# Side steps in another order, q's S1 rows copied from SBUF to SBUF, and the last outputs flushed in another order

## The chip, the cores and the metric

The kernel runs on one core of a Trainium2 chip. The metric is the time of one execution on the device in microseconds (us), the median of several runs. Before the change it is 363.53 us (three runs, 363.38 to 364.76). The engines are TensorE (PE; its weight loads are listed as PEld), VectorE (DVE), ScalarE (ACT), GpSimd (POOL) and SyncE (SP), which here issues the DMA transfers.

## The reference, cut to what matters

A linear attention with a quadratic feature map, and behind it a gated feed-forward block that mixes along the sequence. There are 4 batches, 4 heads, 1088 positions, head size 32 (128 features over the heads), R = 8, 512 gate features.

```python
def phi(x):                                    # 64 features of each position
    a = einsum('rd,bhsd->bhsr', S1, x)
    b = einsum('rd,bhsd->bhsr', S2, x)
    return einsum('bhsi,bhsj->bhsij', a, b).reshape(..., 64)
kv  = einsum('bhsf,bhsd->bhfd', phi(k), v);  z = sum_s phi(k)
x   = einsum('bhsf,bhfd->bhsd', phi(q), kv) / (einsum('bhsf,bhf->bhs', phi(q), z) + 1e-6)
# heads joined: x is [batch, 1088, 128]
h   = gelu(x @ w_in);  u, v = h[..., :512], h[..., 512:]
vn  = (v - mean(v)) / sqrt(var(v) + 1e-6) * g_ln
vs  = einsum('ts,bsd->btd', w_sg, vn) + b_sg[None, :, None]
out = x + (u * vs) @ w_out
```

## The kernel before, in words

Products that need precision are made as three matmuls of float32r halves (high by high, low by high, high by low). A few are plain float32 matmuls.

The work is a chain of batches. For each batch the **main loop** (`Gate.main`) goes over four feature blocks `db` of 128 and three chunks `ci` of the sequence (364, 362 and 362 columns). For each pair it makes `unit` (u, lines 380 to 382), and accumulates the spatial mixing over nine tiles `t` of the sequence in one PSUM bank (`pz`: lines 363, 365 and 371, 26 matmuls). Then `scale` (line 392) and `gate` (lines 400 to 406) make the gated product and its halves gh and gl on DVE and ACT. The gated product is put on a list `pend`; at `t == FL` (7) of each pair, the oldest entry is flushed: `out` multiplies it by w_out into `po` (lines 429 to 431). Four entries are on the list at a time. In the last block, `out` also adds x's two halves (lines 437 and 438) and stores the chunk (line 439). The very last pair of the whole program, `self.final`, is made in plain float32 with a joined weight `wf` (line 427) and one addition of a prepared `xs` (line 435).

While the main loop of batch b runs, the **side steps** of batch b + 1 are put between its matmuls (`Side`): `k1`, `k2` and `kv` (the features of k and their sums with v), `load_q`, `q1`, `q2`, `qp2` and `q3` (the features of q by chunk, and x), `v1`, `v2`, `v3` and `split` (the feed-forward's second half, its normalisation, and its halves vh and vl). Each step has a time in the table `FIRST` (batch 1, beside batch 0) or `LATER` (batches 2 and 3). The main loop calls `tick()` between groups of matmuls, and a step is emitted at the tick that its time falls on. The framework's scheduler then orders the instructions of each engine from there, so that a step can end up later than its tick. Batch 0's own first part, the **head**, runs before any main loop; there a list scheduler orders the steps by costs written in the program plus a correction for each of them in the table `HEAD`.

`spread` takes a chunk's 64 projected rows of q, `ab` (32 rows of S1, 32 of S2), and makes two tiles of 128 rows for each pair of heads: in one each S1 row stands 8 times in a row, in the other the 8 S2 rows of a head are repeated. `qp2` then multiplies the two on DVE (line 237), rounds the product on ACT (line 239) and has POOL make the low half (line 240). Before, `spread` writes both repeated forms to DRAM (lines 151 and 156) and loads them back (line 162).

The tiles of one tag share a fixed number of buffers, among them `r` 6, `ea` and `eb` 2, gt 4, gh and gl 3.

Of the kernel before, what the change touches and what calls it, by code (L numbers as in the profile page):

```python
# [9 lines left out]
F32 = mybir.dt.float32  # L10
# [7 lines left out]
B, H, S, D, R = 4, 4, 1088, 32, 8  # L18
P = 128
# [4 lines left out]
NB = DG // P  # L24
CH = [(0, 364), (364, 362), (726, 362)]
CW = 364
# [4 lines left out]
FL = 7  # L31
# [4 lines left out]


FIRST = [
# [6 lines left out]
]  # L45
LATER = [
# [5 lines left out]
]  # L52
HEAD = [
# [14 lines left out]
]  # L68


def f32(ap):
    return ap.bitcast(F32)
# [11 lines left out]
def tile_kernel(ctx: ExitStack, tc: tile.TileContext, qd, kd, vd, sd, wd, bd, wind, gd, woutd, identd, outd):  # L84
    nc = tc.nc
    mm = nc.tensor.matmul
    V, A, G = nc.vector, nc.scalar, nc.gpsimd
    load = nc.sync.dma_start

    cpool = ctx.enter_context(tc.tile_pool(name="const", bufs=1))  # L90
    dram = ctx.enter_context(tc.tile_pool(name="dram", bufs=1, space=bass.MemoryType.DRAM))
    psum = ctx.enter_context(tc.tile_pool(name="ps", bufs=3, space=PSUM))

    def const(shape, name, dt=F32):
        return cpool.tile(shape, dt, name=name)
# [35 lines left out]
    wout_h = const([P, NB, C], "wout_h", F32R)  # L131
    wout_l = const([P, NB, C], "wout_l", F32R)
# [14 lines left out]

    def spread(pool, ab, cw, name):

        d = dram.tile([2, 2, P, 3 * P], F32, tag="e", name=name + "d", bufs=3)  # L150
        load(
            d[0].rearrange("p (x j) c -> (p x) j c", j=R)[:, :, :cw],
            ab[:32, :cw].unsqueeze(1).broadcast_to([32, R, cw]),
        )
        for p in range(2):
            load(
                d[1, p].rearrange("(i x) c -> x i c", i=R)[:, :, :cw],
                ab[32 + 16 * p : 48 + 16 * p, :cw].unsqueeze(1).broadcast_to([16, R, cw]),
            )
        e = [pool([P, 2, 3 * P], "e" + x, name + x) for x in "ab"]  # L160
        for i in range(2):
            load(e[i][:, :, :cw], d[i].rearrange("p q c -> q p c")[:, :, :cw])
        return e

    class Attention:
# [108 lines left out]
    class Gate:  # L274
# [122 lines left out]
        def gate(self, pool, gt, u, db, ci):  # L397
            c0, cw = CH[ci]
            with tc.high_priority(AHEAD):
                V.tensor_mul(gt, gt, u)  # L400
                if (db, ci) == self.final:
                    return self, db, ci, gt, None
                gl = pool([P, CW], "gl", f"gl{self.b}_{db}_{ci}", F32R)[:, :cw]
                gh = pool([P, CW], "gh", f"gh{self.b}_{db}_{ci}", F32R)[:, :cw]
                A.copy(gh, gt)  # L405
                V.tensor_sub(gl, gt, f32(gh))  # L406
            return self, db, ci, gh, gl

        def end(self, db, ci):

            self.final = db, ci
            xh, xl = self.x
            c0, cw = CH[ci]
            self.wf = self.pool([P, C], "wf", "wout_f")
            V.tensor_add(self.wf, f32(wout_h[:, db]), f32(wout_l[:, db]))
            self.xs = self.pool([P, 512], "r", "x_f")[:, :cw]
            V.tensor_add(self.xs, f32(xh[:, c0 : c0 + cw]), f32(xl[:, c0 : c0 + cw]))

        def out(self, pool, db, ci, gh, gl):
            if db == 0 and ci == 0:  # L420
                self.po = [bank(f"po{self.b}_{c}", f"po{c}", 1) for c in range(3)]
            xh, xl = self.x
            c0, cw = CH[ci]
            cs = slice(c0, c0 + cw)
            o = self.po[ci][:, :cw]
            if (db, ci) == self.final:
                mm(o, lhsT=self.wf, rhs=gh, start=False, stop=True)
            else:
                mm(o, lhsT=wout_h[:, db], rhs=gh, start=(db == 0), stop=False)  # L429
                mm(o, lhsT=wout_l[:, db], rhs=gh, start=False, stop=False)  # L430
                mm(o, lhsT=wout_h[:, db], rhs=gl, start=False, stop=(db == NB - 1))  # L431
            if db == NB - 1:
                ot = pool([P, CW], "gt", f"o{self.b}_{ci}")[:, :cw]
                if (db, ci) == self.final:
                    V.tensor_add(ot, o, self.xs)
                else:
                    V.tensor_add(ot, o, f32(xh[:, cs]))
                    V.tensor_add(ot, ot, f32(xl[:, cs]))
                load(outd[self.b, :, cs], ot)

        def main(self, pool, tick, first, pend, extra=()):
            extra = list(extra)
            if first == 1:
# [3 lines left out]
                for i in range(2 * NT):  # L447
                    t = i % NT
# [8 lines left out]
                for ci in range(len(CH)):  # L457
                    gt = self.scale(pool, zs[ci], 1, ci)
                    u = us.pop() if us else self.unit(pool, 1, ci)
                    pend.append(self.gate(pool, gt, u, 1, ci))  # L460
                first = 2
            for db in range(first, NB):
                for ci in range(len(CH)):
                    cw = CH[ci][1]
                    u = self.unit(pool, db, ci)
                    z = bank(f"pz{self.b}_{db}_{ci}", "psn", 2)[:, :cw]
                    for t in range(NT):
                        self.spatial_h(z, db, ci, t)
                        self.spatial_l(z, db, ci, t)
                        if db + 1 < NB and ci == 0 and t in (1, 3, 5):  # L470
                            run(self.split(db + 1, 3 * (t // 2), 3))
                        if t == FL and pend:
                            flush(pool, *pend.pop(0))
                        if t in EX and extra:
                            extra.pop(0)()
                        if t < NT - 1:
                            tick()
                    pend.append(self.gate(pool, self.scale(pool, z, db, ci), u, db, ci))
                    tick()
# [135 lines left out]
    class Head:  # L615
# [7 lines left out]
        def load(self, name, kb, f, after=()):  # L623
            self.s.at(name, "SP", 0.47, f, after, late=-kb)
# [366 lines left out]
    pend = []  # L991
# [103 lines left out]
```

## Time and profile before

| | |
|---|---|
| median of 3 runs | 363.53 us (363.38 to 364.76) |
| the profiled execution | 363.2 us, of which 361.4 us are the span of the profile |
| PE busy | 350.6 us, 2022 matmuls |
| PE weight loads busy | 321.6 us |
| DVE / ACT / POOL busy | 249.3 / 162.4 / 22.0 us |
| DMA | 30.18 MB, of which 20.92 MB read from and 8.91 MB written to DRAM |

The profile is of one execution. Times in it count from the start of the span. A row of the timeline gives the start, the duration, the engine, the source line, the operation with its output and inputs, and in brackets how long the engine stood before it and what released it. A row of a group (a line, an operation, a shape) gives the count, the busy sum, the mean in ns, and the idle time before. A row of a stretch gives the busy time and the instruction count of each engine in it (PE, PEld, DVE, ACT, POOL), the granted clock of PE, the busy share of the DMA engines and GB/s. Matmuls are pipelined and their ends are modelled, so a busy PE is not a PE at its peak. A transfer's time to landing runs from its issue to its completion.

### The profile page before, as it was taken

Reading aid. Unit: us, or ns where it says so; the run is one execution under the profiler, and the core shown is the slowest. Engines: PE = TensorE matmul, PEld = TensorE weight load, DVE = VectorE, ACT = ScalarE, POOL = GpSimd, SP = SyncE. Lnnn points to the kernel's source line nnn. Section 1 sums busy time; section 2 is a strip of 40 time slices with the busy share of each in tenths; the row PEclk is TensorE's granted clock in tenths of the full one; section 3 lists DMA queues with packets and bytes.
Section 4 is the critical chain, followed back from the end, with each engine's and each line's share of the span. In section 5 each row is a group of like instructions: output and inputs, shape, how many; then the busy total and the mean of one; then the engine's idle time right before and its main releaser. Section 6 shows DMA issues by size and latency. Waiting matters only on the chain.

```text
span 361.4 us, 5443 instructions
## 1 busy us (share of the span) xinstructions
PE 350.6 (97%) x2022; PEld 321.6 (89%) x2022; DVE 249.3 (69%) x603; ACT 162.4 (45%) x355; POOL 22.0 (6%) x37
## 2 busy tenths in 40 slices
PE   7998999999999999999999999999999999999994
PEld 6875569898989999999898999999998999999993
DVE  4688799975999767636859866553697948553134
ACT  5466861325644963314545682332444593232110
POOL 0003000103101000022020000020202000000000
PEclk9999999999999999999999999999999999999998
DMA  7993000883500034484000007672000001000001
GB/s 228 395 410 120 1 2 21 189 260 82 139 21 2 0 82 130 146 206 170 2 0 0 23 0 166 146 191 78 2 0 1 2 0 38 25 0 2 0 2 62
DMA packets 18121, 30.18 MB, mean 84 GB/s; under 512 B 1968, under 2 KB 15024, under 8 KB 18096
## 3 DMA queue, kind: packets, MB, share of 16 engines
q1 hardware_dynamic: 18096, 29.84, 28.2%
q8 instruction: 16, 0.26, 0.3%
q14 instruction: 9, 0.07, 0.1%
HBM read 20.92 MB, written 8.91 MB: 83 GB/s over the span
## 4 chain that ended last, share of the span: by engine, by line
PE 81%; DVE 9%; ACT 5%; DMA 1%; issue 1%; SPq 1%; POOL 1%; DVEq 0%; ACTq 0%
PE pz L363 18%; PE pz L371 17%; PE pz L365 16%; PE pkv L193 3%; ACT vn L335 2%; PE pz L944 2%; PE pv L287 2%; PE pu L380 2%; PE po L431 2%; PE pk L178 2%; PE po L430 2%; PE po L429 2%; PE pv L288 1%; PE pv L289 1%; PE pu L382 1%; PE pu L381 1%
## 5 line engine op out<-in xcount | busy, mean ns | idle before, releaser
L363 PE MATMUL pz<-w_h,vh 128*128 128x362 f32 (+1 forms) x405 | 134.1, 333 | 0.2
L371 PE MATMUL pz<-w_l,vh 128*128 128x362 f32 (+1 forms) x405 | 129.6, 329 | 0.0
L365 PE MATMUL pz<-w_h,vl 128*128 128x364 f32 (+1 forms) x360 | 118.0, 328 | 0.0
L363 PEld LDWEIGHTS pz<-w_h,vh 128*128 128x128 f32 x405 | 76.0, 188 | 1.9 <-DVE gt L392 0.8
L371 PEld LDWEIGHTS pz<-w_l,vh 128*128 128x128 f32 x405 | 75.5, 188 | 0.3
L365 PEld LDWEIGHTS pz<-w_h,vl 128*128 128x128 f32 x360 | 67.7, 188 | 1.2 <-DVE vl L353 0.4
L392 DVE SCALAR_TENSOR_TENSOR gt<-pz,g_col,b_bc 128x362 f32<-128x362 f32 (+1 forms) x48 | 28.1, 590 | 53.7 <-PE pz L371 53.2
L405 ACT CAST gh<-gt 128x362 fp32r<-128x362 f32 (+1 forms) x47 | 22.9, 494 | 63.3 <-PE po L430 54.7
L385 ACT ACTIVATE u<-pu 128x362 f32<-128x362 f32 (+1 forms) x48 | 22.6, 473 | 23.9 <-PE pu L382 17.3
L335 ACT ACTIVATE vn<-vn,nm,rs 128x512 f32<-128x512 f32 x36 | 27.7, 809 | 9.2 <-DVE nm L330 7.5
L353 DVE TENSOR_TENSOR vl<-vn,vh 128x384 fp32r<-128x384 f32 (+2 forms) x60 | 23.1, 419 | 8.4 <-ACT vh L348 8.3
L400 DVE TENSOR_TENSOR gt<-gt,u 128x362 f32<-128x362 f32 (+1 forms) x48 | 25.7, 541 | 3.2 <-ACT u L385 2.9
L259 DVE RECIPROCAL den<-den 128x362 f32<-128x362 f32 (+1 forms) x9 | 21.8, 2417 | 8.8 <-ACT den L256 8.8
L348 ACT CAST vh<-vn 128x384 fp32r<-128x384 f32 (+1 forms) x63 | 23.1, 419 | 7.1 <-PE pz L371 7.1
L406 DVE TENSOR_TENSOR gl<-gt,gh 128x362 fp32r<-128x362 f32 (+1 forms) x47 | 24.6, 529 | 2.4 <-ACT gh L405 1.8
L292 ACT ACTIVATE vn<-pv 128x512 f32<-128x512 f32 x27 | 16.0, 599 | 14.8 <-PE pv L289 14.6
L944 PE MATMUL pz<-w_f,vn 128*128 128x362 f32 (+3 forms) x54 | 18.0, 476 | 1.4 <-ACT vn L335 1.4
L295 DVE BATCH_NORM_STATS2 st<-vn 128x6 f32<-128x512 f32 x27 | 17.9, 678 | 1.4 <-ACT vn L292 1.2
L944 PEld LDWEIGHTS pz<-w_f,vn 128*128 128x128 f32 (+1 forms) x54 | 9.8, 189 | 8.4 <-ACT vn L335 3.1
L380 PE MATMUL pu<-x_h,win_h 128*128 128x362 f32 (+1 forms) x48 | 16.7, 349 | 0.2 <-ACT u L385 0.2
L141 DVE TENSOR_TENSOR kp<-pk,kb 128x256 f32<-128x256 f32 x27 | 11.2, 421 | 7.8 <-ACT kb L181 5.6
L431 PE MATMUL po<-gl,wout_h 128*128 128x362 f32 (+1 forms) x47 | 15.8, 336 | 0.9 <-DVE gl L406 0.9
(195 smaller groups left out, 525.5 us busy)
## 6 DMA issues: line engine op xcount, KB each, us to landing
w_f<-in_w SPq DMA_DIRECT2D x9, 544.0 KB, 10.5
vx<-in_v SPq DMA_DIRECT2D x8, 288.0 KB, 5.0
k<-in_k SPq DMA_DIRECT2D x3, 576.0 KB, 6.2
out<-o SPq DMA_DIRECT2D x8, 181.0 KB, 3.0
e_0d<-ab SPq DMA_DIRECT2D x3, 364.0 KB, 4.4
e_0d<-ab SPq DMA_DIRECT2D x6, 182.0 KB, 5.2
e_0a<-e_0d SPq DMA_DIRECT2D x3, 364.0 KB, 4.1
e_0b<-e_0d SPq DMA_DIRECT2D x3, 364.0 KB, 4.3
```

The costliest lines, as they stand in the source:

```text
L335: A.activation(self.vn[:, t], self.vn[:, t], AF.Identity, bias=self.nm[:, t : t + 1], scale=self.rs[:, t : t + 1])
L348: A.copy(vh[:, ts], vs[:, ts])
L353: self.last = V.tensor_sub(vl[:, ts], vs[:, ts], f32(vh[:, ts]))
L363: last = mm(z, lhsT=vh[:, t], rhs=w_h[:, t, cs], start=(t == 0), stop=False)
L365: last = mm(z, lhsT=vl[:, t], rhs=w_h[:, t, cs], start=False, stop=False)
L371: mm(z, lhsT=self.parts[db][0][:, t], rhs=w_l[t][:, c0 : c0 + cw], start=False, stop=(t == NT - 1))
L380: mm(pu, lhsT=win_h[:, ws], rhs=xh[:, cs], start=True, stop=False)
L392: V.scalar_tensor_tensor(gt, z, g_col[:, db : db + 1], b_bc[:, c0 : c0 + cw], op0=ALU.mult, op1=ALU.add)
L400: V.tensor_mul(gt, gt, u)
L406: V.tensor_sub(gl, gt, f32(gh))
L431: mm(o, lhsT=wout_h[:, db], rhs=gl, start=False, stop=(db == NB - 1))
L944: return mm(zs[ci], lhsT=g.vn[r, t, :P], rhs=w_f[t][r, c0 : c0 + cw], start=(t == 0), stop=(t == NT - 1),)
```

## The change

Four things are changed together:

- the tables `FIRST`, `LATER` and `HEAD` have other numbers (67, 67 and 228 of them, as before);
- `spread` stores only the 32 S2 rows to DRAM, without repeating them; the S1 rows are copied from `ab` straight to the tile, repeated by the transfer; the S2 rows are repeated by the loads from DRAM;
- in the last block of the last batch, two entries of `pend` are flushed in each of the first two chunks and one in the third, so that two are left behind the last group of matmuls; the last batch's outputs are added in one addition each, with x's halves joined beforehand for all three chunks; the addition of chunk 1 is placed behind the final gate's multiplication on DVE;
- the last output is stored in two halves, one issued by SP and one by ACT.

```diff
 FIRST = [
-    8.367, 12.087, 9.623, 6.432, 6.419, 24.648, 11.799, 24.091, 14.517, 39.473, 17.629, 25.126, 22.662, 41.732,
+    -3.495, 11.694, 4.203, 5.044, 4.638, 28.588, 6.333, 23.954, 9.045, 33.842, 12.162, 19.634, 22.34, 36.212,
...
 LATER = [
-    -2.62, 3.464, 4.391, 10, 5.105, 23.019, 12.475, 12.486, 15.836, 11.397, 21.299, 13.02, 21.662, 15.404,
+    -3.752, 3.464, 4.373, 8.047, 3.772, 22.93, 12.437, 12.448, 17.015, 2.843, 19.477, 13.103, 19.806, 23.485,
...
     def spread(pool, ab, cw, name):
 
-        d = dram.tile([2, 2, P, 3 * P], F32, tag="e", name=name + "d", bufs=3)
-        load(
-            d[0].rearrange("p (x j) c -> (p x) j c", j=R)[:, :, :cw],
-            ab[:32, :cw].unsqueeze(1).broadcast_to([32, R, cw]),
-        )
+        d = dram.tile([32, 3 * P], F32, tag="e", name=name + "d", bufs=3)
+        load(d[:, :cw], ab[32:, :cw])
+        e = [pool([P, 2, 3 * P], "e" + x, name + x) for x in "ab"]
         for p in range(2):
-            load(
-                d[1, p].rearrange("(i x) c -> x i c", i=R)[:, :, :cw],
-                ab[32 + 16 * p : 48 + 16 * p, :cw].unsqueeze(1).broadcast_to([16, R, cw]),
-            )
-        e = [pool([P, 2, 3 * P], "e" + x, name + x) for x in "ab"]
-        for i in range(2):
-            load(e[i][:, :, :cw], d[i].rearrange("p q c -> q p c")[:, :, :cw])
+            load(e[0][:, p, :cw], ab[16 * p : 16 * p + 16, :cw].unsqueeze(1).broadcast_to([16, R, cw]))
+        for p in range(2):
+            load(e[1][:, p, :cw], d[16 * p : 16 * p + 16, :cw].unsqueeze(0).broadcast_to([R, 16, cw]))
         return e
...
         def gate(self, pool, gt, u, db, ci):
             c0, cw = CH[ci]
             with tc.high_priority(AHEAD):
-                V.tensor_mul(gt, gt, u)
+                made = V.tensor_mul(gt, gt, u)
                 if (db, ci) == self.final:
+                    self.gated = made.ins
                     return self, db, ci, gt, None
...
             self.wf = self.pool([P, C], "wf", "wout_f")
             V.tensor_add(self.wf, f32(wout_h[:, db]), f32(wout_l[:, db]))
-            self.xs = self.pool([P, 512], "r", "x_f")[:, :cw]
-            V.tensor_add(self.xs, f32(xh[:, c0 : c0 + cw]), f32(xl[:, c0 : c0 + cw]))
+            self.xs = []
+            for c0, cw in CH:
+                self.xs.append(self.pool([P, 512], "r", f"x_f{c0}")[:, :cw])
+                V.tensor_add(self.xs[-1], f32(xh[:, c0 : c0 + cw]), f32(xl[:, c0 : c0 + cw]))
...
             if (db, ci) == self.final:
                 mm(o, lhsT=self.wf, rhs=gh, start=False, stop=True)
+                ot = pool([P, CW], "gt", f"o{self.b}_{ci}")[:, :cw]
+                V.tensor_add(ot, o, self.xs[ci])
+                n = cw // 2
+                load(outd[self.b, :, c0 : c0 + n], ot[:, :n])
+                A.dma_start(outd[self.b, :, c0 + n : c0 + cw], ot[:, n:])
+                return
...
             if db == NB - 1:
                 ot = pool([P, CW], "gt", f"o{self.b}_{ci}")[:, :cw]
-                if (db, ci) == self.final:
-                    V.tensor_add(ot, o, self.xs)
+                if self.final:
+
+                    with tc.issue_after(self.gated) if ci == 1 else ExitStack():
+                        V.tensor_add(ot, o, self.xs[ci])
                 else:
                     V.tensor_add(ot, o, f32(xh[:, cs]))
                     V.tensor_add(ot, ot, f32(xl[:, cs]))
...
-                        if t == FL and pend:
+
+                        few = self.final and db == NB - 1
+                        if t == FL and len(pend) > (1 if few and ci == 2 else 0) or t == 3 and few and len(pend) > 1:
                             flush(pool, *pend.pop(0))
```

More of the change, by code (lines that the diff above doesn't have):

```diff
@@ L412, in end @@
             xh, xl = self.x
-            c0, cw = CH[ci]
             self.wf = self.pool([P, C], "wf", "wout_f")
             V.tensor_add(self.wf, f32(wout_h[:, db]), f32(wout_l[:, db]))
-            self.xs = self.pool([P, 512], "r", "x_f")[:, :cw]
-            V.tensor_add(self.xs, f32(xh[:, c0 : c0 + cw]), f32(xl[:, c0 : c0 + cw]))
+            self.xs = []
+            for c0, cw in CH:
+                self.xs.append(self.pool([P, 512], "r", f"x_f{c0}")[:, :cw])
+                V.tensor_add(self.xs[-1], f32(xh[:, c0 : c0 + cw]), f32(xl[:, c0 : c0 + cw]))
         def out(self, pool, db, ci, gh, gl):
@@ L427, in out @@
                 mm(o, lhsT=self.wf, rhs=gh, start=False, stop=True)
[L428 to L431, printed above, removed]
+                ot = pool([P, CW], "gt", f"o{self.b}_{ci}")[:, :cw]
[4 more added lines that the diff above has]
+                return
+            mm(o, lhsT=wout_h[:, db], rhs=gh, start=(db == 0), stop=False)
+            mm(o, lhsT=wout_l[:, db], rhs=gh, start=False, stop=False)
+            mm(o, lhsT=wout_h[:, db], rhs=gl, start=False, stop=(db == NB - 1))
             if db == NB - 1:
                 ot = pool([P, CW], "gt", f"o{self.b}_{ci}")[:, :cw]
-                if (db, ci) == self.final:
-                    V.tensor_add(ot, o, self.xs)
+                if self.final:
+                    with tc.issue_after(self.gated) if ci == 1 else ExitStack():
+                        V.tensor_add(ot, o, self.xs[ci])
                 else:
```

48 rows, old and new, of tables (FIRST, HEAD, LATER) are left out of this document.

## The prediction

> **What bounds the kernel now.** I read the page first (span and engine totals), then the busy time in four stretches, then the matmul groups by form, then the waits and the timeline where the tensor engine (PE) stands, and the last ten microseconds.
>
> ```profile
> span 361.4 us, 5443 instructions
> PE 350.6 (97%) x2022; PEld 321.6 (89%) x2022; DVE 249.3 (69%) x603; ACT 162.4 (45%) x355; POOL 22.0 (6%) x37
> ```
>
> ```profile
> 0.00:53.00 53.00, 49.26 (x243) 34.84 (x244) 40.29 (x123) 33.96 (x60) 3.45 (x18) 1.00 0.53 197
> 53.00:295.00 242.00, 240.13 (x1418) 226.77 (x1417) 180.12 (x418) 111.45 (x258) 18.59 (x19) 1.00 0.30 77
> 295.00:355.00 60.00, 60.00 (x362) 59.64 (x361) 26.36 (x58) 16.97 (x38) 0.00 (x0) 1.00 0.03 10
> 355.00:361.40 6.40, 1.19 (x4) 0.37 (x3) 2.50 (x6) 0.00 (x0) 0.00 (x0) 0.85 0.25 87
> ```
>
> ```profile
> L193 PE MATMUL pkv<-vx,kp 128*128 128x128 f32 x108 | 14.7, 276 | 0.4 <-DVE gt L392 0.4
> L287 PE MATMUL pv<-win_h,x_h 128*128 128x512 f32 x27 | 11.4, 435 | 0.1
> L178 PE MATMUL pk<-sk,k 128*128 128x128 f32 x54 | 10.2, 282 | 0.1
> ```
>
> ```profile
> 131.96 1.79 PE pkv L193 x16
> ```
>
> The program keeps PE busy 97% of the span at a granted clock of 1.00. The busy share overstates it, since a 362-column matmul is shown as 0.33 us and the next starts half that later. The stretch 295:355, the last batch with no side steps beside it, gives the pace: 60.00 / 362 = 0.166 us a matmul. I price the stretch 53:295 by that. Its 1418 matmuls are 108 (L193) and 54 (L178) small ones at 1.79 / 16 = 0.112 us, 3 x 27 = 81 of 512 columns (L287 to L289) at 0.166 x 512 / 362 = 0.234, and 1175 others at 0.166: 18.1 + 19.0 + 195.1 = 232.2 us. The stretch took 242.0. So about 10 us of it are starts that came late: a wait, and the weight load that a wait exposes. That is the whole pool from which another order of side steps can draw. The rest of the span is the head (53 us, ordered by its own table) and the tail after the last gate.
>
> **Side steps: FIRST and LATER.** Nothing is computed more or less often; the numbers say after which tick of the main loop a step is put in. A tick is two or three matmul groups of the main loop, and I turned both tables into ticks. In FIRST (batch 1's steps beside batch 0) the k projections 0, 1, 3, 4, 5 come 4 to 6 ticks earlier, the projections of q's first two chunks 4 earlier, the products of chunk 0 go from tick 17 to 4 and 9, one product of chunk 1 from 21 to 17, the sums k2(4) to k2(8), kv and q3(0) 4 earlier, the normalisation v2(0) 10 earlier, and the last v1, v3 and splits later. In LATER the moves are small: up to 5 ticks in the first half, and v1(4) onward with v2 and v3 mostly 5 to 14 later. The longest wait of PE in these stages is this one:
>
> ```profile
> 87.60 0.97 POOL L240 TENSOR_TENSOR qpl<-e_1a,qph 128x362 fp32r<-128x362 f32 x1 [3.54 <-ACT qph L239]
> 87.63 1.33 DVE L237 TENSOR_TENSOR e_1a<-e_1a,e_1b 128x362 f32<-128x362 f32 x1
> ...
> 89.33 1.42 DVE L406 TENSOR_TENSOR gl<-gt,gh 128x362 fp32r<-128x362 f32 x3
> ...
> 89.91 0.43 PE L431 MATMUL po<-gl,wout_h 128*128 128x362 f32 x1 [0.85 <-DVE gl L406]
> ```
>
> ```profile
> 80.68 0.98 DVE L237 TENSOR_TENSOR e_0a<-e_0a,e_0b 128x364 f32<-128x364 f32 x2
> ...
> 83.15 1.30 DVE L237 TENSOR_TENSOR e_1a<-e_1a,e_1b 128x362 f32<-128x362 f32 x1
> ```
>
> A product of two spread tiles takes 0.98 / 2 = 0.49 us on DVE alone, but 1.33 us at 87.63, where POOL's subtraction L240 runs from 87.60. The gate's multiplication and its low half gl queue behind it, and PE waits 0.85 us for gl. It is the second of chunk 1, 4.5 us after the first (83.15), and so falls among the gates. With one of chunk 1's products asked for 4 ticks earlier, chunk 0's earlier still, and the operands there sooner (next part), I take this wait as gone: -0.85. Late next is the gate's own chain, which is shorter by that product. A second wait is at the end of block 1:
>
> ```profile
> 68.50 0.60 DVE L392 SCALAR_TENSOR_TENSOR gt<-pz,g_col,b_bc 128x364 f32<-128x364 f32 x1 [0.32 <-PE pz L371]
> ...
> 69.15 0.94 PE L193 MATMUL pkv<-vx,kp 128*128 128x128 f32 x6 [0.35 <-DVE gt L392]
> ```
>
> PE has finished the block, takes up k2, and stands for 0.35 us until DVE is through the scaling L392. The new table puts two of these sums earlier (tick 9 for 10) and two later (22 for 19). I credit half, and as much again for the small waits of L178 on its copies: -0.4 together. In batches 2 and 3 PE stands where ACT is in the middle of side steps; this piece of the chain of work is one, an activation that PE's next projection waits for:
>
> ```profile
> 174.74 0.48 ACT u L385
> ```
>
> The later v3 and splits spread ACT's work over more of the block. The waits there are small and many, so no single row prices them: by the pool of 10 us, from 0 to half of what those two batches hold (some 7 of the 10 if it is shared out by time, 168 of 242 us), and a gain is not certain either, so from +1 to -3.5. I take -0.75, nearer to none, since the moves are small. Side steps together: -0.85 - 0.4 - 0.75 = -2.0.
>
> **Spread.** Before, a chunk takes 5 transfers: one broadcast of the S1 rows to DRAM (L151), two of the S2 rows (L156), and two reloads (L162) that wait for them. After, also 5: one small store of the 32 S2 rows without copies, two broadcasts of the S1 rows straight to the tile, two broadcasting reloads of the S2 rows. Bytes written fall from 4 x 364 KB to 46 + 2 x 364 KB (32 rows are an eighth of 364 KB).
>
> ```profile
> 62.68 0.68 SPq L151 DMA_DIRECT2D e_0d<-ab  x1
> 63.41 2.00 SPq L156 DMA_DIRECT2D e_0d<-ab  x2
> 66.74 0.43 SPq L162 DMA_DIRECT2D e_0a<-e_0d  x1
> ...
> 69.51 0.38 SPq L162 DMA_DIRECT2D e_0b<-e_0d  x1
> ```
>
> ```profile
> e_0b<-e_0d SPq DMA_DIRECT2D x1, 364.0 KB, 5.0
> ```
>
> ```profile
> DMA to landing us min/median/max: 3.3/4.3/5.5
> ```
>
> Before, from the first issue to the last landing: 69.51 + 5.0 - 62.68 = 11.8 us. After: the small store lands after 1.9 to 3.0 (bounded by the stores of 181 KB, rows at the tail below), meanwhile SP issues two broadcasts of 0.6 to 1.0 us each, then two reloads, the last issue 3 to 4 us in, landing 3.3 to 5.5 later (L162's landing row, of all reloads): 6.3 to 9.5, I take 7.8, so 4 us sooner. SP's queue carries only loads and stores for later batches behind it, and its occupation falls or stays (5 issues either way). No engine's busy time changes, so by itself this is worth 0: its cover is the 6 us between e_0b's landing at 74.5 and its product at 80.68. Its worth is that the product at 87.63 can go ahead, priced above. If it is not faster, that 0.85 is at risk.
>
> The Trainium skill speaks against it. Its page DMA: Bandwidth & Descriptors, in Rules for kernel authors (the goal of using all 16 engines), says that a leading zero-stride broadcast of c copies confines the whole DMA to at most c engines; the S2 reload leads with a broadcast of 8. By the rule each half would run on 8 engines, twice the bytes per engine. No run so far shows such a reload.
>
> **Head.** I worked the new table through the ordering routine for the order alone. SP and POOL keep theirs. On DVE, kv goes ahead of two products and three neighbouring pairs swap; on PE, k2(8) goes ahead of two q projections and two pairs of v1 swap; on ACT, the copies for w_h of tiles 2 and 3 change places, and v3(1) goes ahead of gelu(5).
>
> ```profile
> PE pz L944 <- ACT vn L335: 1.4, 2, 1.2
> ```
>
> ```profile
> L335 ACT ACTIVATE vn<-vn,nm,rs 128x512 f32<-128x512 f32 x36 | 27.7, 809 | 9.2 <-DVE nm L330 7.5
> ```
>
> PE's longest wait in the head is 1.2 us for the first normalised tile; its predecessors (bn, norm) keep their places. So 0, with bounds of -1.2 (that wait gone) and +0.8 (one vn of 0.81 us put in front of what PE waits for).
>
> **Tail.** Before, each of the last block's three groups of matmuls flushes one entry, and four are left when the last group ends; after, the first two flush two each and the last one, and two are left. Six matmuls move ahead of the last gate. Outputs 0 and 1 are then added with one addition each (the sum of x's halves is made beforehand, two more DVE additions in a stretch where DVE is busy 26 of 60 us), and the last store is halved over SP and ACT.
>
> ```profile
> 353.43 0.32 PE L371 MATMUL pz<-w_l,vh 128*128 128x362 f32 x1
> ...
> 355.33 0.88 PE L427 MATMUL po<-gt,wout_f 128*128 128x362 f32 x2
> ```
>
> ```profile
> 353.79 0.59 DVE L392 SCALAR_TENSOR_TENSOR gt<-pz,g_col,b_bc 128x362 f32<-128x362 f32 x1 [3.85 <-PE pz L371]
> 354.30 0.53 DVE L406 TENSOR_TENSOR gl<-gt,gh 128x362 fp32r<-128x362 f32 x1
> 354.74 0.53 DVE L400 TENSOR_TENSOR gt<-gt,u 128x362 f32<-128x362 f32 x1
> 355.19 0.97 DVE L437 TENSOR_TENSOR o<-po,x_h 128x364 f32<-128x364 f32 x2
> ...
> 356.97 0.53 DVE L435 TENSOR_TENSOR o<-po,x_f 128x362 f32<-128x362 f32 x1
> ```
>
> ```profile
> 356.63 1.29 SPq L439 DMA_DIRECT2D out<-o  x3
> ```
>
> ```profile
> out<-o SPq DMA_DIRECT2D x8, 181.0 KB, 3.0
> ```
>
> ```profile
> SPq L1091 <- DMA out<-o: 1.9, 1, 1.9
> ```
>
> PE pays nothing in total, but the last gate starts 6 x 0.166 = 1.0 later: L392 at 354.79. It gets that back: gl is done by then, so L400 follows after 0.51 (from L392 to the next in the rows) at 355.30; the final matmul 0.59 after L400's start (355.33 - 354.74) at 355.89, ending at 356.77; the last addition 0.04 on (as L392 after L371) at 356.81, since only one other addition, placed behind L400, precedes it. Before, it stood until 356.97 behind four. So -0.16 only. The half stores are bounded by the 1.9 us wait after the last issue: by bytes it could halve (-0.9); a second queue and its wait could add 0.3. I take -0.15. Tail: -0.3.
>
> **Sum.** -2.0 + 0 + 0 - 0.3 = -2.3. The profiled execution took 363.2 us, 1.8 outside its span, so 360.9; the median of the runs shown is 363.53, 0.3 above it, so 361.2.
>
> **Rivals.**
> 1. The waits only change places: the pool of 10 us is many starts of a tenth, each tied to a queue in which DVE or ACT work must be somewhere. For it: DVE is busy 180 of 242 us there whatever the order. Against: the 0.85 wait has one nameable cause. Time: 363.5 - 0.3 = 363.2.
> 2. The spread is no faster. If the S2 reload's two halves run on half of the engines one behind the other, each takes as long as a whole reload now (4.3 us): 4 + 2 x 4.3 = 12.6 us for 11.8. Then the product stays at 87 us and its 0.85 is kept: 361.2 + 0.85 = 362.1. The rule above would do this.
> 3. Half the pool goes: -5.0 - 0.3, 358.2.
> 4. Slower. DVE is the full engine at the switch to batch 0's second block:
>
> ```profile
> 53.00:73.00 20.00, 19.65 (x127) 18.77 (x126) 19.49 (x32) 5.00 (x16) 1.00 (x1) 1.00 0.45 106
> ```
>
> ```profile
> 65.97 1.27 DVE L958 TENSOR_TENSOR w_l<-w_f,w_h 64x1088 fp32r<-64x1088 f32 x1
> ...
> 67.79 1.00 PE L371 MATMUL pz<-w_l,vh 128*128 128x362 f32 x5
> ```
>
> DVE makes the low halves w_l there, the last from 65.97 to 67.24. The last three L371 need it, at 67.79 + 2 x 0.166 = 68.12, so 0.9 us of slack. With q2(0) at tick 3 instead of 7 (27 ticks in the some 15 us of block 1, so 2.2 us sooner; the first issue at 60.5 instead of 62.68) and a spread of 7.8 us, operands land by about 68, and k's products are asked for sooner as well. Four products ahead of w_l or vl cost 2.0 us clean and 5.3 at 1.33 each; less the slack, +1.1 to +4.4. A product at the head of DVE's queue whose operand has not landed holds up w_l, gt and gl the same way. It decides from 3.0 us of such time before 68 us (0.9 slack and 2.1 for a slower kernel): then about 366.0. Against it: an operand that lands at 68 comes too late to be ahead of most of w_l.
>
> **Chances.** What a measurement can tell from no change is about 0.5%, 1.8 us. Forecast 0.50 (its own range 359.8 to 362.5; four fifths of it below 361.7), rival 1 0.20, rival 2 0.06, rival 3 0.12, rival 4 0.12. Faster by more than 0.5%: 0.40 + 0.12 = 0.52; within: 0.10 + 0.20 + 0.06 = 0.36; slower: 0.12. The range goes from the upper part of rival 3 to above rival 1 and the cheap end of rival 4 (363.5 + 1.1 - 0.3): 358.7 to 364.4, leaving out rival 4's dear part and the lower half of rival 3, 0.18.
>
> **What would show it.** Right: no wait of PE near 0.85 us for gl in batch 0; the products of chunk 1 done before 85 us; first issue to last landing of a spread near 8 us; the stretch 53:295 shorter by 1 to 3 us at the same number of matmuls; the last addition about 3.5 us after the last L371 plus the same 3.9 us end, with two stores at the end. Wrong: w_l later than 67.2 us with L371 waiting for it; products of 1.3 us among the gates elsewhere; the last store landing later than 1.9 us after its issue.

## The result, and the profile after

The changed kernel takes 367.98 us (median of 4 runs, 366.49 to 369.04): 1.0112 of the kernel before, interval 1.0069 to 1.0155. It is slower by 4.5 us (367.98 against 363.50, the median of four runs of the kernel before beside it), where 361.2 was forecast. Its profiled execution took 367.61 us, and its span is 4.2 us longer than before (365.6 for 361.4). One run of the experiments, 380.36 us of the kernel before with the new spread and the products held, lies 1.9% above the fastest of its kernel at a lower granted clock and is left out of that kernel's figures below. The page's first rows of after, and the stretches of it (columns as in the prediction):

```profile
span 365.6 us, 5440 instructions
PE 348.6 (95%) x2022; PEld 323.6 (89%) x2022; DVE 253.2 (69%) x603; ACT 163.2 (45%) x355; POOL 22.5 (6%) x37
```

```profile
0.00:53.00 53.00, 49.29 (x243) 34.85 (x244) 40.07 (x123) 33.98 (x60) 3.46 (x18) 1.00 0.53 197
53.00:295.00 242.00, 233.53 (x1389) 223.86 (x1388) 184.66 (x422) 114.26 (x263) 19.08 (x19) 0.99 0.21 51
225.00:245.00 20.00, 16.78 (x100) 16.12 (x99) 11.19 (x23) 5.63 (x14) 2.89 (x3) 0.91 0.46 104
245.00:300.00 55.00, 55.00 (x320) 53.14 (x320) 42.55 (x105) 29.23 (x62) 3.26 (x3) 1.00 0.01 1
```

The head is the same: 243 matmuls to 53 us in both. In 53:295 there are 1389 matmuls where there were 1418: 29 x 0.166 = 4.8 us are lost there. From 245 on PE runs without a break. So the loss lies between 53 and 245, and the waits of after say where:

```profile
DVE e_0a L233 <- DMA e_0b<-e_0d: 6.2, 4, 4.2
PE pz L359 <- DVE gt L388: 5.6, 2, 3.0
DVE e_1a L233 <- DMA e_1b<-e_1d: 5.3, 3, 2.9
```

Before, the only wait of PE for the scaling was the one of 0.35 us ahead of k2, which is still there, and no product (L237 then, L233 now) waited for a transfer. The timeline of DVE and of PE at the first of PE's two waits:

```profile
140.35 0.54 DVE L233 TENSOR_TENSOR e_0a<-e_0a,e_0b 128x364 f32<-128x364 f32 x1 [4.24 <-DMA e_0b<-e_0d]
141.05 0.54 DVE L233 TENSOR_TENSOR e_0a<-e_0a,e_0b 128x364 f32<-128x364 f32 x1 [0.17 <-DMA e_0b<-e_0d]
141.51 0.59 DVE L388 SCALAR_TENSOR_TENSOR gt<-pz,g_col,b_bc 128x362 f32<-128x362 f32 x1
```

```profile
142.15 0.43 PE L359 MATMUL pz<-w_h,vh 128*128 128x362 f32 x1 [2.98 <-DVE gt L388]
```

Two products of q's features stand at the head of DVE's queue. The first waits 4.24 us for its operand. Behind it stands the scaling L388, which reads the sum that PE has finished out of its bank, and PE waits 2.98 us for it. The second place is the same with chunk 1 of batch 3, and there more is lost than the wait:

```profile
239.31 0.54 DVE L233 TENSOR_TENSOR e_1a<-e_1a,e_1b 128x362 f32<-128x362 f32 x1 [2.87 <-DMA e_1b<-e_1d]
239.76 0.59 DVE L388 SCALAR_TENSOR_TENSOR gt<-pz,g_col,b_bc 128x364 f32<-128x364 f32 x1
```

```profile
237.50 0.33 PE L378 MATMUL pu<-x_l,win_h 128*128 128x362 f32 x1
240.41 0.67 PE L359 MATMUL pz<-w_h,vh 128*128 128x362 f32 x1 [2.59 <-DVE gt L388]
240.87 0.51 PE L361 MATMUL pz<-w_h,vl 128*128 128x362 f32 x1
...
243.29 0.43 PE L359 MATMUL pz<-w_h,vh 128*128 128x362 f32 x1
243.55 0.32 PE L361 MATMUL pz<-w_h,vl 128*128 128x362 f32 x1
```

From 237.50 to 240.41 are 2.91 us for one matmul, so 2.75 lost. Then the ten starts to 243.55 take 3.14 us instead of 1.66: the clock is granted at half there (0.91 over the 20 us in the row above), another 1.5. Together 2.98 + 2.75 + 1.5 = 7.2 us, more than the 4.8 missing: by this estimate the rest of the change gained about 2.4 us in these stages.

### The profile page after: what moved, and what is told of

It reads as the page before. It is cut to its first block, busy times and chain, and to the rows that moved or that the text cites. A ratio compares the mean times of both kernels' runs of the same rounds, so it can differ in the third digit from the quotient of the medians.

```text
span 365.6 us, 5440 instructions
## 1 busy us (share of the span) xinstructions
PE 348.6 (95%) x2022; PEld 323.6 (89%) x2022; DVE 253.2 (69%) x603; ACT 163.2 (45%) x355; POOL 22.5 (6%) x37
## 4 chain that ended last, share of the span: by engine, by line
PE 68%; DVE 11%; DMA 11%; ACT 3%; SPq 3%; issue 2%; POOL 1%; DVEq 0%; ACTq 0%
PE pz L359 15%; PE pz L367 15%; PE pz L361 13%; DMA e_1b<-e_1d 3%; DMA e_0b<-e_0d 3%; DMA vx<-in_v 2%; PE pz L951 2%; PE pu L376 2%; PE pkv L189 2%; PE po L432 2%; PE po L434 2%; PE po L433 2%; PE pu L378 2%; PE pu L377 2%; DMA e_0d<-ab 2%
## 5 line engine op out<-in xcount | busy, mean ns | idle before, releaser
L367 PE MATMUL pz<-w_l,vh 128*128 128x362 f32 (+1 forms) x405 | 130.1, 330 | 0.0
L367 PEld LDWEIGHTS pz<-w_l,vh 128*128 128x128 f32 x405 | 75.9, 189 | 0.2
L388 DVE SCALAR_TENSOR_TENSOR gt<-pz,g_col,b_bc 128x362 f32<-128x362 f32 (+1 forms) x48 | 28.3, 592 | 34.0 <-PE pz L367 33.6
L396 DVE TENSOR_TENSOR gt<-gt,u 128x362 f32<-128x362 f32 (+1 forms) x48 | 26.6, 554 | 0.3
L344 ACT CAST vh<-vn 128x384 fp32r<-128x384 f32 (+1 forms) x63 | 24.0, 418 | 0.8 <-PE pz L367 0.8
L288 ACT ACTIVATE vn<-pv 128x512 f32<-128x512 f32 x27 | 15.8, 594 | 14.3 <-PE pv L285 12.2
L252 ACT ACTIVATE den<-pnd,eps_t 64x362 f32<-64x362 f32 (+1 forms) x18 | 10.1, 560 | 17.3 <-PE pnd L248 15.5
L189 PE MATMUL pkv<-vx,kp 128*128 128x128 f32 x108 | 15.5, 278 | 1.2 <-DVE kp L143 0.8
```

The source lines that it names most:

```text
L344: A.copy(vh[:, ts], vs[:, ts])
L367: mm(z, lhsT=self.parts[db][0][:, t], rhs=w_l[t][:, c0 : c0 + cw], start=False, stop=(t == NT - 1))
L388: V.scalar_tensor_tensor(gt, z, g_col[:, db : db + 1], b_bc[:, c0 : c0 + cw], op0=ALU.mult, op1=ALU.add)
L396: made = V.tensor_mul(gt, gt, u)
```

## The experiments

Theory A: all of the loss is the position of the products on DVE. They stand ahead of work that PE needs soon, and their operands land later than that. Rival B: another part of the change costs it. All ratios are against the kernel before on the same chip (medians 362.97 to 363.24 us).

| kernel | median us | ratio, interval |
|---|---|---|
| after, old spread | 377.74 | 1.0403, 1.0385 to 1.0421 |
| before, new spread | 380.11 | 1.0474, 1.0437 to 1.0511 |
| before, new last outputs | 363.48 | 1.0008, 0.9998 to 1.0018 |
| after, products held behind the scaling | 361.16 | 0.9948, 0.9935 to 0.996 |
| before, new spread, products held | 374.76 | 1.0325, three runs from 1.028 to 1.0374 |
| after, rows by way of DRAM, products held | 363.42 | 1.0015, 0.9988 to 1.0042 |
| after, rows by way of DRAM | 369.83 | 1.0178, 1.014 to 1.0216 |
| before, products held | 363.28 | 1.0008, 0.9998 to 1.0018 |
| products held behind k's features | 361.56 | 0.997, 0.9953 to 0.9987 |
| products held, old LATER | 366.13 | 1.0092, 1.0063 to 1.0121 |
| products held, old last outputs | 362.02 | 0.9967, 0.9954 to 0.998 |
| products held behind both | 360.90 | 0.9926, 0.9912 to 0.994 |

### Products behind the scaling

```diff
     def qp2(self, j):
...
-            V.tensor_mul(a, a, b)
+            with tc.issue_after(scaled[-1]) if self.b > 1 else ExitStack():
+                V.tensor_mul(a, a, b)
...
     def scale(...):
-                V.scalar_tensor_tensor(gt, z, ...)
+                scaled.append(V.scalar_tensor_tensor(gt, z, ...).ins)
```

> The changed kernel with each product of batches 2 and 3 held on DVE behind the scaling issued last before it; nothing else is moved by hand. Theory A: the two waits of PE for a scaling go, 360.5 to 362.5 us, with the spread's transfers as slow as now (about 8.7 us from first issue to landing). Rival C (traffic): the SBUF-to-SBUF copies cost time wherever the products stand: still 365 us or more.

361.16 us (360.95 to 362.33), 6.8 less than after, or 6.0 by the two ratios, with no transfer and no table changed. In the two traces PE's 2022 matmuls stand in the same order, and so do SP's transfers; what differs is the order of DVE, and of the casts on ACT that follow the products. The DVE timeline at the first place, and the stretch there:

```profile
138.75 0.59 DVE L389 SCALAR_TENSOR_TENSOR gt<-pz,g_col,b_bc 128x362 f32<-128x362 f32 x1 [2.24 <-PE pz L368]
139.85 0.54 DVE L234 TENSOR_TENSOR e_0a<-e_0a,e_0b 128x364 f32<-128x364 f32 x1 [0.50 <-DMA e_0b<-e_0d]
```

```profile
136.00:142.00 6.00, 6.00 (x40) 6.00 (x39) 3.26 (x7) 1.08 (x3) 0.95 (x1) 1.00 0.54 130
```

The scaling goes first, the product still waits for its landing, and PE is busy throughout. The product is not later than in after (139.85 against 140.35). At the second place the scaling goes first too, but now k's features stand behind a product that waits, and PE behind them:

```profile
237.90 0.54 DVE L234 TENSOR_TENSOR e_1a<-e_1a,e_1b 128x362 f32<-128x362 f32 x1 [3.30 <-DMA e_1b<-e_1d]
```

```profile
239.27 1.16 PE L189 MATMUL pkv<-vx,kp 128*128 128x128 f32 x8 [1.63 <-DVE kp L143]
```

Theory A is shown: both waits for the scaling and the stretch at half clock are gone with the order of DVE, and 6.0 to 6.8 of the 7.2 us came back. The rest is no more than this new wait.

### One part of the change at a time

```diff
 # after, old spread: FIRST, LATER, HEAD and the outputs as changed
     def spread(pool, ab, cw, name):
-        d = dram.tile([32, 3 * P], ...)
...
+        d = dram.tile([2, 2, P, 3 * P], ...)      # the five transfers of before
 # before, new spread: the reverse
 # before, new last outputs: FIRST, LATER, HEAD and spread as before
```

> The changed kernel with the old spread (both forms through DRAM); tables and last outputs stay changed. Theory A (products): the new spread lets the products of q's tiles stand on DVE ahead of a gate's scaling before their operands have landed, and the two waits of PE that follow (2.98 and about 2.75 us) and the 3.4 us at half clock behind the second (1.7 us) are 7.4 us, which hide a gain of about 3 by the rest. With the old spread the products stand behind those scalings again: 360.0 to 361.5 us, no wait of PE over 1 us in batches 1 and 2's main loops. Rival B (tables): the new order of the side steps is itself the loss: 365 us or more. Rival D (last outputs on two queues): 365 us or more too, with the loss after the last group.

> The kernel before with the new spread alone. Theory A: products again stand ahead of scalings, waits of PE of 1 to 3 us for the scaling behind a product that waits for a landing: 365 to 369 us. Rival B: no loss, within 1 us of before (363.5).

> The kernel before with the new last outputs alone (old tables, old spread). By the traces the stretch from the last group's last matmul to the end fell from 7.97 to 6.52 us for 1.0 us more ahead of it: 0.4 us faster than before, 363.1. Rival D: slower than before.

Old spread under the new tables: 377.74, a miss by 17 us and the strongest sign that the parts do not add. Rival B's bound (365 or more) is met, but the products stand behind the scalings as theory A had it, and it is other steps that come late. New spread under the old tables: 380.11, right in sign, 11 us too small in size. Three waits of PE for the scaling are there, 6.9 us in all, as theory A had it; a gate's cast (2.6 us), the kv table (1.9) and k's features (1.7) come late besides. Together the two parts cost some 4 us, each alone 15 to 17. The outputs alone change nothing that can be told.

The same tables put the steps at other times when the transfer is another. This is chunk 0 of batch 2, in after and then with the old spread: the first issue of the spread on SP, and the product.

```profile
132.25 0.33 SPq L153 DMA_DIRECT2D e_0d<-ab  x1
```

```profile
139.40 0.56 SPq L153 DMA_DIRECT2D e_0d<-ab  x1
```

```profile
159.65 0.98 DVE L239 TENSOR_TENSOR e_0a<-e_0a,e_0b 128x364 f32<-128x364 f32 x2
```

The numbers of the tables are identical, yet the product stands at 159.65 instead of 140.35. So a table's time does not fix the place on DVE; it goes with what the framework's scheduler takes the transfer to need (no run shows how it estimates that). With the old spread, batch 1's last chunk is late the same way. Its reciprocal stands at 118.26 (2.42 us), where after has it at 104.32. Its x is then too late for PE:

```profile
119.55 0.33 PE L440 MATMUL po<-gl,wout_h 128*128 128x364 f32 x1
123.65 0.76 PE L289 MATMUL pv<-win_h,x_h 128*128 128x512 f32 x1 [3.77 <-DVE h L317]
```

```profile
119.00:130.00 11.00, 7.23 (x24) 6.00 (x23) 8.44 (x25) 3.76 (x7) 0.00 (x0) 0.69 0.00 0
```

The releaser named (h, at 123.42) is only the last record of DVE before it; the matmul reads x_h, whose last part DVE copies at 123.32, and the next one x_l, copied at 123.49.

### Old tables, or old LATER, with the products held

```diff
 # before, new spread, products held: FIRST, LATER and HEAD of before, new spread,
 # and the hold of the version above
 # products held, old LATER: the version above with LATER of before
```

> The kernel before with the new spread (380.1 us by itself), and with each product of batches 2 and 3 held on DVE behind the newest gate scaling. Theory A (a product that is placed ahead of its landing is the whole loss, the side-step tables are worth little): 361 to 365. Theory C (the tables are planned for the operands' new times, and without them other steps collide too): 368 to 376, since only the waits on products, 6.9 us, and one or two stretches at half clock (1.7 us each) go.

> The version with the products held (361.2 us), with the table of ticks LATER (the side steps issued from batch 1's main part on) as it was before; FIRST and HEAD as changed. If the side-step tables and the new spread only work together, this loses what the old tables lost in batches 2 and 3: 365 to 372. Rival (only FIRST matters, whose steps run while the first batch is on): 361 to 363.

374.76 and 366.13: theory C in the first, the tables and the spread working only together in the second. The new tables are worth some 14 us with this spread (374.76 - 361.16 = 13.6; the last outputs differ too, by some tenths), and the old LATER alone costs 5.0. Holding the products does not heal the old tables, since other work stands ahead of its landing too. ACT of the first of the two:

```profile
76.95 0.49 ACT L213 CAST qt_0h<-q 128x364 fp32r<-128x364 f32 x1 [4.08 <-DMA q<-in_q]
77.35 0.49 ACT L400 CAST gh<-gt 128x364 fp32r<-128x364 f32 x1
```

```profile
77.89 0.67 PE L424 MATMUL po<-gh,wout_h 128*128 128x364 f32 x1 [2.72 <-ACT gh L400]
```

It is the same mechanism on another engine: a cast of q waits 4.08 us for q's load, the gate's cast gh stands behind it, and PE waits 2.72 us. With LATER of before alone it is a product of chunk 2 that waits, with the cast of the kv table behind it on DVE, and PE behind that:

```profile
243.59 0.54 DVE L233 TENSOR_TENSOR e_2a<-e_2a,e_2b 128x362 f32<-128x362 f32 x1 [2.44 <-DMA e_2b<-e_2d]
244.04 0.29 DVE L203 CAST kv_h<-kv 128x256 fp32r<-128x256 f32 x1
```

```profile
244.47 0.92 PE L246 MATMUL pnd<-qph,kv_h 128*128 128x364 f32 x2 [2.46 <-DVE kv_h L203]
```

### Is it the transfer's speed?

```diff
-        d = dram.tile([32, 3 * P], ...)
-        load(d[:, :cw], ab[32:, :cw])
+        d = dram.tile([64, 3 * P], ...)
+        load(d[:, :cw], ab[:, :cw])
...
-            load(e[0][:, p, :cw], ab[16 * p : 16 * p + 16, :cw].unsqueeze(1)...)
+            load(e[0][:, p, :cw], d[16 * p : 16 * p + 16, :cw].unsqueeze(1)...)
...
-            load(e[1][:, p, :cw], d[16 * p : 16 * p + 16, :cw].unsqueeze(0)...)
+            load(e[1][:, p, :cw], d[32 + 16 * p : 48 + 16 * p, :cw].unsqueeze(0)...)
```

The copy out of SBUF is slow: the packet records of after give 218 ns for one of its packets of 1456 bytes, and 62 ns for the same packet in the reload from DRAM. Two stretches of after, the copy (with the reload's first packets at its end) and the reload:

```profile
134.50:136.50 2.00, 2.00 (x14) 2.00 (x14) 1.61 (x5) 0.50 (x1) 0.00 (x0) 1.00 0.91 117
139.00:140.00 1.00, 0.17 (x2) 0.00 (x0) 0.00 (x0) 0.00 (x0) 0.00 (x0) 1.00 0.54 199
```

The copy keeps 0.91 of the 16 DMA engines busy for 117 GB/s, the reload moves 199 with 0.54 of them, some eight. So all rows were sent by way of DRAM, with and without the hold:

> The changed kernel with the products of batches 2 and 3 held behind the newest scaling (361.2 us), and S1's rows stored to DRAM once as S2's are and spread from there. Theory A (the broadcast out of SBUF is what is slow, 218 ns a packet against 62): the last landing of a spread 1.0 to 1.5 us sooner, the wait of 1.79 us at 237 about halved, 360.0 to 361.0. Rival (the copies cost what their bytes cost, and the store of twice the rows eats the rest): landing within 0.5 us, 361.0 to 362.5.

> The changed kernel with S1's rows stored to DRAM once and spread from there, products not held. Theory A: a landing 1.0 to 1.5 us sooner shortens the product's waits of 4.24 and 2.87 us by so much, and no stretch at half clock follows: 363 to 365. Rival (the framework's own model of the transfer moves the products too, and they come before their landing all the same): 366 to 370.

With the hold 363.42 (ten runs from 360.77 to 365.89), above both ranges; without it 369.83, as the rival had it. It is no better either way. SP of the held one shows why:

```profile
132.45 0.51 SPq L153 DMA_DIRECT2D e_0d<-ab  x1
136.18 1.20 SPq L156 DMA_DIRECT2D e_0a<-e_0d  x2
```

All four loads now wait 3.7 us for the store, and the product starts at 141.55, where it started at 139.85 with the copies out of SBUF. Here the chain of store and loads counted for more than the packets. Without the hold, the product waits 5.39 us and PE stands from 139.44 to 142.66.

### The prediction's own wait, and the outputs

```diff
 # before, products held: qp2 of before, held from batch 1 on
-            V.tensor_mul(a, a, b)
+            with tc.issue_after(scaled[-1]) if self.b > 0 else ExitStack():
+                V.tensor_mul(a, a, b)
 # products held, old last outputs: out, flush and the last store as before
```

> The kernel before with nothing else than its products of batches 1, 2 and 3 held behind the newest gate scaling. The prediction's step (a wait of 0.85 us for gl behind a product at 87.63, and some of the 0.75 in batches 2 and 3): 362.4 to 363.0. Rival (the wait changes place, as its first rival had it): 363.3 to 364.0.

> The version with the products held (361.2 us), with the last outputs in the order of before. The prediction's term (the new order saves 0.3 us): 361.3 to 361.8. Rival (as in the kernel before, where the new outputs alone made no difference that could be told): 361.0 to 361.3.

Before with its products held: 363.28, no change. The hold moved nothing, since the scalings stood ahead of these products already; the late start at the prediction's place is still there (1.03 us at 89.80). So this run says nothing on what taking that wait away is worth, and that stays open. The old outputs in the held version: 362.02, above both ranges, but 0.9967 against 0.9948 with intervals that overlap, so no more than some tenths can be claimed for the new ones.

### Behind k's features, and behind both

```diff
-            with tc.issue_after(scaled[-1]) if self.b > 1 else ExitStack():
-                V.tensor_mul(a, a, b)
+            with ExitStack() as held:
+                for ins in (scaled[-1], made_k[-1]) if self.b > 1 else ():
+                    held.enter_context(tc.issue_after(ins))
+                V.tensor_mul(a, a, b)
```

`made_k` holds the instructions of `features`. In the first of the two kernels there was one list for both kinds, so a product stood behind the newer of the two only.

> The version with the products of batches 2 and 3 held behind the newest gate scaling (361.2 us), with each of them held behind the newest product of k's features as well. There TensorE waited 1.79 us at 237 for k's features, which stood on DVE behind a product that waited 3.30 us for its landing. Theory A (what stands behind a product that waits for its landing pays): that wait goes, 359.4 to 360.6. Rival (q's features are then late for the numerator, or the wait changes place): 361.0 to 362.0.

> The version with the products of batches 2 and 3 held behind the newest gate scaling (361.2 us), held behind the newest product of k's features besides, so that neither stands behind a product whose operand is under way. Against holding behind the features alone (361.6 us, with a wait of 1.60 us at 138 for a scaling behind a product): that wait goes, 359.8 to 360.8. Rival (the landing sets the end whatever waits behind it: 1.9 us at 157 for the kv table stay or grow): 361.0 to 362.0.

Behind the newest of either kind: 361.56, no gain over 361.16. The wait at 237 went, but a product came ahead of a scaling again (1.60 us at 138.43), and PE was 1.92 us late for the kv table at 156.63. Behind both: 360.90 (360.36 to 361.74), a tenth above theory A's range. It is the lowest median, 0.9926 of the kernel before, though its interval (0.9912 to 0.994) still touches that of the first held version (0.9935 to 0.996). The waits at 138 and 237 are gone. What is left of the mechanism in it, on DVE and PE:

```profile
156.35 0.98 DVE L239 TENSOR_TENSOR e_1a<-e_1a,e_1b 128x362 f32<-128x362 f32 x2 [3.34 <-DMA e_1b<-e_1d]
157.25 0.42 DVE L202 TENSOR_TENSOR kv<-pkv,ident 128x256 f32<-128x256 f32 x1
157.71 0.89 DVE L207 CAST kv_h<-kv 128x256 fp32r<-128x256 f32 x1
```

```profile
158.74 0.58 PE L252 MATMUL pnd<-qph,kv_h 128*128 128x364 f32 x2 [1.96 <-DVE kv_h L207]
```

The kv table now stands behind the waiting products, which the rival had named; so part of the price stays.

## Why the prediction was wrong

**The step that failed** is the one that gave the spread "by itself" the worth 0, with "the 6 us between e_0b's landing at 74.5 and its product at 80.68" as its cover, and that saw the spread's worth only in a product that "can go ahead". Both took the product to stay behind its landing. It did not. Chunk 0 of batch 2, before:

```profile
130.81 0.56 SPq L151 DMA_DIRECT2D e_0d<-ab  x1
...
142.33 0.38 SPq L162 DMA_DIRECT2D e_0b<-e_0d  x1
```

```profile
154.53 0.98 DVE L237 TENSOR_TENSOR e_0a<-e_0a,e_0b 128x364 f32<-128x364 f32 x2
```

This last load landed 4.3 us after its issue, at 146.6, and the product came 7.9 us behind it. In after the last landing is at 141.05, 5.6 us sooner, but DVE reaches the product at 136.1 (140.35 less the wait of 4.24), 18 us sooner. The cover of 7.9 us was used up, and DVE stood for 4.2 us. At the second place the landing is not sooner at all (239.3 in after, 239.0 before: issue at 234.90 and 4.1 us), and the product still starts 13.7 us earlier (239.31 for 253.00). I turned the tables into ticks and read ticks as places; a place comes from the tables and the transfer together, as the old spread under the new tables showed.

**Rival 4 had the mechanism and the wrong place.** One of its sentences is what happened ("A product at the head of DVE's queue whose operand has not landed holds up w_l, gt and gl the same way"), but I priced it at 68 us in batch 0 only. There nothing happened. The last w_l stands at 65.97 as before, and the products at 67.17 without a wait. I never carried it to batches 2 and 3, where it cost 7.2 us.

**Side steps, -2.0.** The wait of 0.85 us for gl is gone and chunk 1's products are done before 85 us (75.56 and 80.65), as said. But PE is as late near the same time for a sum's bank (x L259), which stands behind a reciprocal:

```profile
86.11 2.42 DVE L255 RECIPROCAL den<-den 128x364 f32<-128x364 f32 x1
```

```profile
88.99 0.33 PE L361 MATMUL pz<-w_h,vl 128*128 128x362 f32 x1
90.00 0.41 PE L246 MATMUL pnd<-qph,kv_h 128*128 128x362 f32 x1 [0.68 <-DVE x L259]
```

From 88.99 to 90.00 are 0.85 us above the pace, so rival 1 held there: the wait changed place. The 0.35 us in front of k2 is still 0.35 (at 69.35). The gain of about 2.4 us that after hides, and the 1.8 to 2.3 that the held versions keep (361.16 against 362.99, and 360.90 against 363.24 of the runs beside it), came from elsewhere in the blocks. It is near the -2.0 by size, which is luck, since it did not come at the places I named; where it came from is open. (The upper end of the range, 363.5 + 1.1 - 0.3, is 364.3 and not 364.4; nothing hangs on it.)

**Spread, 7.8 us.** It took 8.8 for chunk 0 of batch 2 (132.25 to 141.05), where it took 15.8 before (130.81 to 146.6; the 11.8 is that of a chunk of batch 1), so rival 2 did not come. The Trainium skill's page DMA: Bandwidth & Descriptors, in Rules for kernel authors, has a DMA with a leading broadcast of c copies confined to at most c engines, here 8; the reload's share of 0.54 of the 16 agrees.

**Head, 0:** right, 243 matmuls to 53.00 and the main loop's first at 53.20 in both. **Tail, -0.3:** the last addition starts 2.5 us after the last L367 of the gate, which is 1.0 later, so 3.5 in all, as said. The two traces differ by -0.45 from the last steady matmuls to the end. But by themselves the new outputs gave 1.0008 (0.9998 to 1.0018): a term that the timing cannot tell from nothing.

```profile
359.08 0.32 PE L367 MATMUL pz<-w_l,vh 128*128 128x362 f32 x1
...
361.58 0.54 DVE L427 TENSOR_TENSOR o<-po,x_f 128x362 f32<-128x362 f32 x1 [0.52 <-PE po L425]
```

## What to carry to other kernels

An instruction that waits for a transfer costs nothing until something that the busy engine needs stands behind it in the same in-order queue. When a transfer gets quicker, ask first whether its consumer will be moved forward by more than the landing, and look at what stands behind it. An order tuned against one transfer belongs to that transfer: change either alone and both must be planned again, or the consumer tied behind the work that must not wait.

## What the runs showed of the hardware

A wait can cost more than itself. In after PE stood idle for 2.98 us ahead of 142.15 and for 2.59 us ahead of 240.41. Behind the first the clock was granted in full, behind the second at half from 240.08 to 243.49. With the old tables and the products held, an idle time of 1.75 us (ahead of 172.28) had half clock behind it:

```profile
142.00:146.00 4.00, 3.85 (x25) 3.85 (x26) 3.06 (x6) 0.75 (x3) 1.43 (x2) 1.00 0.00 0
240.08:243.49 3.41, 3.08 (x10) 3.08 (x11) 1.59 (x4) 0.49 (x1) 0.96 (x1) 0.50 0.66 124
```

```profile
173.41:176.82 3.41, 3.41 (x13) 3.10 (x12) 3.20 (x4) 2.80 (x7) 0.00 (x0) 0.50 0.00 0
```

Both stretches are 3.41 us long, and between their starts and that of the half clock after the last matmul lies a whole number of steps of 3.41 us (240.08 to 362.96 is 36 of them, 173.41 to 367.97 is 57). So in these traces the clock changes at the ends of steps that do not begin with a gap. Counted back from 240.08, a step ends at 141.09 and cuts the first gap into 1.9 and 1.1 us. The second gap has 2.25 us of its idle time in one step (236.67 to 240.08), and the 1.75 us lie in one too (170.00 to 173.41). That the cut saved the first gap is argued, not shown: a step with 1.9 us of idle time had no half clock behind it and one with 1.75 us had, so the idle time within a step does not settle it alone.

The Trainium skill's page TensorE: Matmul & The Clock Gate, in Part 1 on the clock gate, has the activity watched in free-running windows of about 3.4 us. The steps above agree with that. Its table has the clock at half after at least one idle window; that 1.75 us of idle time suffice does not fit it.

The steps could also be why after's runs spread over 2.5 us: the two longer ones (368.35 and 369.04) have a mean granted clock of 0.988 and 0.987, the two shorter (366.49 and 367.61) 0.992, and one more step at half clock would lower the mean by 0.0047 (an estimate, 3.41 x 0.5 / 366). No run here tests it.
